# The last inverse DFT of a gated FFT mixer in two halves of 256 columns in place of two quarters and a half, with the MLP's result added sooner

## The chip, the cores and the metric

One core of one Trainium2 chip runs the whole kernel in one launch. The metric is the device time of that launch in microseconds, and a change counts as faster or slower when it moves the time by over 2%. In a profile the span, from the first to the last instruction, is some 2 us shorter than the time of the same run.

The engines are named as the profile names them: PE is TensorE (matmuls), PEld its weight loads, DVE is VectorE, ACT is ScalarE, POOL is GpSimd, SP is SyncE, whose queue issues the transfers. PSUM is the memory that matmuls write to; it has eight banks of 128 x 512 f32.

## The reference

A row of 512 features is mixed in two ways and the two results are blended with a gate. One way is a global filter (a 2D FFT over the 2048 rows and 512 features, a product with a complex weight, and the inverse FFT); the other is an MLP with the Mish activation.

```python
x = A_x                                              # 1 x 2048 x 512, bf16
g = sigmoid((x * gate_w).sum(-1, keepdims=True))
X = rfft2(x)                                         # over rows and features
a = irfft2(X * (w_r + 1j * w_i), (2048, 512)).astype(bf16)
h = einsum("bsd,df->bsf", x, w1) + b1                # 512 -> 1792
b = einsum("bsf,fd->bsd", h * tanh(softplus(h)), w2) # 1792 -> 512
out = g * a + (1 - g) * b
```

## The kernel before

The kernel is a list of small tasks (`G.add`). Each has one or two possible engines with an estimated duration, the tiles that it reads and writes, and a priority. A scheduler in the program puts them in order on each engine before anything is built, so the order of instructions follows from the list and its estimates; every engine then runs its list strictly in that order. The rows are 16 tiles of 128 (`t`).

The DFTs are matmuls with constant matrices. The forward part, the complex product (with a shuffle through DRAM on either side) and the MLP's first products come first. The stage that matters here is the last one, which runs beside the MLP. For each tile it does:

- the inner product (`s1i`): four matmuls of 128 columns against GT, into one PSUM bank;
- a copy of that bank to SBUF as bf16 (`e5`, tile TT), on ScalarE or VectorE;
- the outer product (`a1i`): matmuls of TT against GD, the inverse DFT along the features, into one PSUM bank (`sy`);
- the gate and the sum with the MLP's tile.

The inverse DFT along the features is folded. The frequencies k fall into even ones, with sum E, and odd ones, with sum O; both are needed for n < 256 only, as y(n) = E(n) + O(n) and y(n + 256) = E(n) - O(n). Before the change E is folded a second time: the frequencies that are multiples of four give C0 and the others C2, for n < 128 only, and E is C0 + C2 on the first 128 columns and C0 - C2 on the next. So the bank `sy` holds C0 (128 columns), C2 (128) and O (256).

```python
# inner product: weights are strided slices of T2r, 128 columns of GT move through
for i in range(4):
    st_ = T2r[:, 2*t:2*t+2, 2*i::4] if i < 2 else T2r[:, 2*t+i-2, 1::2]
    ins = e.matmul(ps[:, bk(sk), 128*i:128*(i+1)], st_, GT[:, t, :], start=True, stop=True)
... # e5: TT <- that bank
# outer product
for i in range(2):
    e.matmul(o[:, 128*i:128*i+128], TT[:, st.i, i, :], GD[:, 128*i:128*i+128], start=True, stop=True)
e.matmul(o[:, 256:512], TT[:, st.i, 2, :], GD[:, 256:512], start=True, stop=False)
return e.matmul(o[:, 256:512], TT[:, st.i, 3, :], GD[:, 512:768], start=False, stop=True)
...
# ge, on ScalarE (or VectorE):  tE[256:384] = g * C0
# ee, VectorE, twice 128:       tE[0:128] = g * C2 + g * C0 ; tE[128:256] = -g * C2 + g * C0
# yr, VectorE, twice 256:       d = g * O + tE ; d' = -g * O + tE
#     t < NEARLY (early): d is a bf16 scratch tile tA;  else d is the output tile ya
# yb, VectorE, early tiles only: ya = ya + tA
```

A tile of the MLP's result reaches the output in one of two ways. In an early tile (`t < NEARLY`, 12 of 16 before) the task `bev` copies the MLP's PSUM bank to `ya`, scaled with 1 - g (`omg`), and the filter's part is added later (`yb`). In a late tile the filter's part is in `ya` first, and the task `fo` adds the MLP's bank: `ya = omg * bank + ya`, on VectorE. The MLP's second product is `mm2` (14 matmuls of 512 columns per tile, in two groups of seven), its first one `mm1` (groups of four).

```python
fpool = _Pool(4)     # four PSUM banks for s1i and a1i together
mpool = _Pool(4)     # four for the MLP
ttpool, tepool = _Pool(3), _Pool(3)     # three TT and three tE tiles
```

Of the kernel before, what the change touches and what calls it, by code (L numbers as in the profile page):

```python
# [7 lines left out]
BF = mybir.dt.bfloat16  # L8
F32 = mybir.dt.float32
AF = mybir.ActivationFunctionType  # L10
ALU = mybir.AluOpType

S, D, F = 2048, 512, 1792
# [3 lines left out]
BIAS = 0.15  # L17
NWARM = 14
NTR = 4
NEARLY = 12  # L20


BGRP = {1: (0, 2), 3: (2, 2), 7: (4, 4), 11: (8, 4), 15: (12, 4)}
# [164 lines left out]
def _build_consts():  # L188
    cs = {}
    n = np.arange(128)[:, None]  # L190
    q = np.arange(64)[None, :]

    def trig(nn, k):
        th = 2 * np.pi * nn * k / D
        return np.cos(th), -np.sin(th)

    c0, s0 = trig(n, 4 * q)
    s0[:, 0] = (-1.0) ** np.arange(128)
    c2, s2 = trig(n, 4 * q + 2)
    ko = np.concatenate([4 * q + 1, 4 * q + 3], axis=1)  # L200
    blocks = [c0, s0, c2, s2]
    for h in range(2):
        c1, s1 = trig(n + 128 * h, ko)
        blocks += [c1, s1]
    cs["FD"] = np.concatenate(blocks, axis=1)

    p = np.arange(128)[:, None]
    e = np.arange(64)[None, :]
    FT = np.zeros((128, NT, 128))
    GT = np.zeros((128, NT, 128))  # L210
    for t in range(NT):
        th = 2 * np.pi * e * (16 * p + t) / S
        FT[:, t, 0:64] = np.cos(th)
        FT[:, t, 64:128] = -np.sin(th)
        FT[:, t, 64] = (-1.0) ** p[:, 0]
        GT[0:64, t, :] = 2 * np.cos(th).T
        GT[64:128, t, :] = -2 * np.sin(th).T
        GT[0, t, :] = 1.0
        GT[64, t, :] = (-1.0) ** p[:, 0]
    cs["CF"] = np.concatenate([cs.pop("FD"), FT.reshape(128, NT * 128)], axis=1)  # L220
    cs["GT"] = GT


    GD = np.zeros((128, 768))
    n1, n2 = np.arange(128)[None, :], np.arange(256)[None, :]
    for i in range(2):
        th = 2 * np.pi * (4 * np.arange(64)[:, None] + 2 * i) * n1 / D
        GD[0:64, 128 * i:128 * i + 128] = 2 * np.cos(th)
        GD[64:128, 128 * i:128 * i + 128] = -2 * np.sin(th)
    GD[0, 0:128] = 1.0  # L230
    GD[64, 0:128] = (-1.0) ** np.arange(128)
    th = 2 * np.pi * (2 * np.arange(128)[:, None] + 1) * n2 / D
    GD[:, 256:512] = 2 * np.cos(th)
    GD[:, 512:768] = -2 * np.sin(th)
    cs["GD"] = GD / (S * D)
    cs["SM"] = _stage2()
    return cs
# [162 lines left out]
PR = dict(ld=100.0, tr=99.5, a1=98.0, s1=99.0, mid=96.0, fin=94.0, mm1=80.0, act=90.0, mm2=70.0, out=95.0, gate=99.8, cp=95.5, gx=97.0)  # L400


def _build(nc, A_x, A_w_r, A_w_i, B_w1, B_b1, B_w2, gate_w, out):
# [5 lines left out]
    G = _Graph()  # L409
    es = ExitStack()  # L410
    with es:
        def sb(name, shape, dt):
            return es.enter_context(nc.sbuf_tensor(name, shape, dt))
# [8 lines left out]
        hsb = sb("hsb", [128, 3, NFT, 512], BF)  # L422
        CF = sb("CF", [128, 768 + NT * 128], BF)
        FD = CF[:, 0:768]
        GD = sb("GD", [128, 768], BF)
        FT = CF[:, 768:].rearrange("p (t e) -> p t e", t=NT)
        GT = FT
        SM = sb("SM", [128, len(MATS), 128], BF)
# [4 lines left out]
        PX = PXf.bitcast(BF)  # L433
# [14 lines left out]
        Xb = PX[:, 0:1024].rearrange("p (i k) -> p i k", i=2)  # L448
        P1 = PX[:, 1024:2048].rearrange("p (i k) -> p i k", i=2)
        P2 = PX[:, 2048:3072].rearrange("p (i k) -> p i k", i=2)  # L450
        tA = PX.rearrange("p (i k) -> p i k", i=3)
        tE = PXf[:].rearrange("p (i k) -> p i k", i=3)
        x_sb = R1[:].rearrange("p (t d) -> p t d", t=NT)
        In2 = R2[:].rearrange("p (j k) -> p j k", j=32)
# [36 lines left out]
        def bk(s):  # L491
            return s.i if s.pool is fpool else 4 + s.i
# [14 lines left out]
        def pe_dur(ncols, nmm=1):  # L507
            return nmm * max(ncols / 2400.0 + 0.003, 0.057)

        def act_dur(n, ptr=False):  # L510
            return 0.17 + n * 0.000833 + (0.09 if ptr else 0.0)

        def dve_dur(n, rate=1.0, ptr=False):
            return 0.15 + n * 0.001042 / rate + (0.06 if ptr else 0.0)
# [17 lines left out]
        G.add("eul", [("pool", 0.2, lambda e: e.memset(eul[:, :], float(np.e)))], writes=["eul"], prio=99)  # L532


        G.add("zero", [("dve", 0.2, lambda e: e.memset(GD[:, 0:512], 0.0))], writes=["GD"], prio=100)  # L535
        sl = fslot()
        for i in range(NWARM):
            G.add(f"warm{i}", [("pe", 0.42 if i < 5 else 0.22, lambda e, sl=sl: e.matmul(ps[:, bk(sl), :], GD[:, 0:128], GD[:, 0:512], start=True, stop=True))],  # L538
                  reads=["GD"], writes=[sl], slots=[sl] if i == 0 else (), prio=-100.0)


# [178 lines left out]

        for t in range(8, NT):
            ld_xt(t, t_r1r)
        dma("ld_gd", GD[:], d_c["GD"][:], 128 * 1536, writes=["GD"], deps=t_r1r)
        dma("ld_gt", GT, d_c["GT"][:], 128 * 4096, writes=["GT"], deps=t_s1 + t_r1r)


# [151 lines left out]
        for t in range(NT):  # L878
            sk = fslot()

            def f_s1i(e, t=t, sk=sk):
                ins = None
                for i in range(4):
                    st_ = T2r[:, 2 * t:2 * t + 2, 2 * i::4] if i < 2 else T2r[:, 2 * t + i - 2, 1::2]
                    ins = e.matmul(ps[:, bk(sk), 128 * i:128 * (i + 1)], st_, GT[:, t, :], start=True, stop=True)  # L885
                return ins

            G.add(f"s1i_{t}", [("pe", pe_dur(128, 4), f_s1i)], reads=[("T2r", t // 4), "GT"], writes=[sk], slots=[sk], deps=t_a1i[t - 3:t - 2] if t > 2 else (), prio=PR["fin"])
            st = _Slot(ttpool)

            def f_e5(e, sk=sk, st=st):
                return e.tensor_copy(out=TT[:, st.i, :, :].rearrange("p a b -> p (a b)"), in_=ps[:, bk(sk), :])  # L892

            def f_e5a(e, sk=sk, st=st):
                return e.activation(TT[:, st.i, :, :].rearrange("p a b -> p (a b)"), ps[:, bk(sk), :], AF.Copy)  # L895

            G.add(f"e5_{t}", [("dve", dve_dur(512), f_e5), ("act", act_dur(512), f_e5a)], reads=[sk], writes=[st], slots=[st], prio=PR["fin"] + 0.2)
            sy = fslot()

            def f_a1i(e, st=st, sy=sy):  # L900
                o = ps[:, bk(sy), :]
                for i in range(2):
                    e.matmul(o[:, 128 * i:128 * i + 128], TT[:, st.i, i, :], GD[:, 128 * i:128 * i + 128], start=True, stop=True)  # L903
                e.matmul(o[:, 256:512], TT[:, st.i, 2, :], GD[:, 256:512], start=True, stop=False)  # L904
                return e.matmul(o[:, 256:512], TT[:, st.i, 3, :], GD[:, 512:768], start=False, stop=True)  # L905

            t_a1i.append(G.add(f"a1i_{t}", [("pe", pe_dur(128, 2) + pe_dur(256, 2), f_a1i)], reads=[st, "GD"], writes=[sy], slots=[sy], prio=PR["fin"] + 0.3))
            se = _Slot(tepool)
            G.add(f"ge_{t}", [("act", act_dur(128, True), lambda e, t=t, sy=sy, se=se: e.activation(tE[:, se.i, 256:384], ps[:, bk(sy), 0:128], AF.Copy, scale=gcol[:, t:t + 1])),  # L909
                              ("dve", dve_dur(128, ptr=True), lambda e, t=t, sy=sy, se=se: e.tensor_scalar(  # L910
                                  out=tE[:, se.i, 256:384], in0=ps[:, bk(sy), 0:128], scalar1=gcol[:, t:t + 1], scalar2=None, op0=ALU.mult))],
                  reads=[sy, "gcol"], writes=[se], slots=[se], prio=PR["fin"] + 0.4)

            def f_ee(e, t=t, sy=sy, se=se):
                for o, g in ((0, gcol), (128, ngcol)):
                    ins = e.scalar_tensor_tensor(out=tE[:, se.i, o:o + 128], in0=ps[:, bk(sy), 128:256], scalar=g[:, t:t + 1], in1=tE[:, se.i, 256:384], op0=ALU.mult, op1=ALU.add)
                return ins

            G.add(f"ee_{t}", [("dve", 2 * dve_dur(128, ptr=True), f_ee)], reads=[sy, "gcol", "ngcol"], writes=[se], prio=PR["fin"] + 0.4)
            early = t < NEARLY  # L920

            def f_yr(e, t=t, sy=sy, se=se, early=early):
                for o, g in ((0, gcol), (256, ngcol)):
                    d = tA[:, se.i, 512 + o:768 + o] if early else ya[:, t, o:o + 256]
                    ins = e.scalar_tensor_tensor(out=d, in0=ps[:, bk(sy), 256:512], scalar=g[:, t:t + 1], in1=tE[:, se.i, 0:256], op0=ALU.mult, op1=ALU.add)  # L925
                return ins

            G.add(f"yr_{t}", [("dve", 2 * dve_dur(256, ptr=True), f_yr)], reads=[sy, "gcol", "ngcol"] + ([] if early else [se]),
                  writes=[se] if early else [("ya", t)], deps=t_r1w, prio=PR["fin"] + 0.4)
            if early:  # L930
                G.add(f"yb_{t}", [("dve", dve_dur(512, 2), lambda e, t=t, se=se: e.tensor_tensor(  # L931
                    out=ya[:, t, :], in0=ya[:, t, :], in1=tA[:, se.i, 512:1024], op=ALU.add))],
                      reads=[se, ("b", t)], writes=[("o", t, 0)], prio=PR["fin"] + 0.4)

        for t, n0, n1, sl in late:
            def f_out(e, t=t, sl=sl, n0=n0, n1=n1):
# [116 lines left out]
```

## Time and profile before

| what | before |
|---|---|
| time, median of 3 (lowest, highest) | 135.46 us (135.18, 135.64) |
| span of the profiled execution | 133.5 us |
| TensorE busy | 128.9 us |
| VectorE busy | 99.4 us |
| ScalarE busy | 82.8 us |
| mean TensorE clock, of full | 1.00 |
| copy of a bank after s1i on ScalarE, 128 x 512 | 593 ns |
| scaled copy on ScalarE (`ge`), 128 x 128 | 364 ns |
| `ee`, one of its two, 128 x 128 | 345 ns |
| `yr`, one of its two, 128 x 256 | 484 ns |
| `yb`, 128 x 512, bf16 in and out | 426 ns |
| `fo`, 128 x 512 | 752 ns |

The duration of a matmul in a group is from its start to its modelled end (219 ns for 128 columns), and neighbours overlap. What a matmul costs in a dense stream is read from the distances in the chain of waits, not from that mean. The busy time of a group counts overlaps once.

Lines of the kernel that the profile names: L836 is `mm1`, L858 `mm2`, L869 `bev`, L885 `s1i`, L892 and L895 its copy on VectorE and on ScalarE, L903 to L905 `a1i`, L909 and L910 `ge` on ScalarE and on VectorE, L916 `ee`, L925 `yr`, L931 `yb`, L937 `fo`. L521 and L520 are the copies out of PSUM of the earlier stages, on ScalarE and on VectorE, and L809 is a matmul of the stage before.

### The profile page before, as it was taken

The page shows a single profiled execution, that of the slowest core. Times are in us where ns is not written, and L with a number is a line of the kernel's source. Part 1 is how long each engine was busy: PE and PEld are TensorE (multiplying, and loading weights), DVE is VectorE, ACT ScalarE, POOL GpSimd, SP SyncE. Part 2 cuts the span into 40 slices and gives each one's busy share as a digit, 9 for nine tenths or more (in the row PEclk, how much of TensorE's full clock was granted, in tenths as well). Part 3 has the DMA queues.
Part 4 walks back from the last instruction along what each step waited for, and adds up shares of the span by engine and source line. Part 5 has one row for each costly group of instructions (what it writes and reads, how often), then busy time and mean ns, then how long its engine had stood idle before and what let it go on. Part 6 is the DMA issues. An engine that isn't in the chain of part 4 may idle for free.

```text
span 133.5 us, 2357 instructions
## 1 busy us (share of the span) xinstructions
PE 128.9 (97%) x813; PEld 69.4 (52%) x813; DVE 99.4 (75%) x241; ACT 82.8 (62%) x145; POOL 4.7 (4%) x8
## 2 busy tenths in 40 slices
PE   6999999999999999999998999999999999999991
PEld 2489565675444444444443444445666566565451
DVE  0558868487999799999999995001899999977822
ACT  3199788896774156756167898778887654552000
POOL 2000000000002900000000000000000000000000
PEclk9999999999999999999999999999999999999999
DMA  3999999997999999947100840399311222220121
GB/s 89 289 382 401 329 187 158 190 333 230 254 352 394 383 166 125 140 100 206 49 0 0 323 158 0 158 258 290 80 46 37 79 79 79 79 85 1 43 75 39
DMA packets 25015, 22.24 MB, mean 167 GB/s; under 512 B 7596, under 2 KB 21420, under 8 KB 24876
## 3 DMA queue, kind: packets, MB, share of 16 engines
q1 hardware_dynamic: 24976, 22.10, 62.2%
q8 instruction: 6, 0.10, 0.3%
q14 instruction: 5, 0.04, 0.1%
q10 hardware_dynamic: 28, 0.00, 0.0%
HBM read 14.23 MB, written 6.29 MB: 154 GB/s over the span
## 4 chain that ended last, share of the span: by engine, by line
PE 45%; DVE 5%; issue 1%; ACT 0%; ACTq 0%
PE ps L858 18%; PE ps L836 18%; PE ps L885 3%; PE ps L903 1%; PE ps L904 1%; PE ps L905 1%; PE ps L809 1%; DVE PX L794 1%; DVE PX L793 1%; DVE Wb L692 1%; DVE PX L790 1%; DVE PX L797 1%; PE ps L780 1%; DVE R L520 1%; ACT PX L521 0%
## 5 line engine op out<-in xcount | busy, mean ns | idle before, releaser
L836 PE MATMUL ps<-xT,w_sb 128*128 128x512 bf16 (+1 forms) x240 | 52.3, 365 | 0.1
L858 PE MATMUL ps<-w_sb,hsb 128*128 128x512 bf16 (+2 forms) x238 | 52.3, 366 | 0.0
L845 ACT ACTIVATE hsb<-ps,b1f 128x512 bf16<-128x512 f32 (+1 forms) x60 | 38.9, 660 | 9.4 <-PE ps L836 9.4
L858 PEld LDWEIGHTS ps<-w_sb,hsb 128*128 128x128 bf16 x238 | 22.3, 98 | 22.9
L836 PEld LDWEIGHTS ps<-xT,w_sb 128*128 128x128 bf16 x240 | 22.7, 98 | 22.0 <-issue 0.6
L520 DVE CAST R<-ps 128x512 bf16<-128x512 f32 (+1 forms) x23 | 15.4, 689 | 6.6 <-PE ps L656 3.7
L521 ACT ACTIVATE R<-ps 128x512 bf16<-128x512 f32 (+1 forms) x25 | 14.4, 595 | 3.1 <-PE ps L809 2.1
L869 ACT ACTIVATE R<-ps,omg 128x512 bf16<-128x512 f32 x12 | 8.1, 687 | 9.2 <-PE ps L858 8.1
L521 ACT ACTIVATE PX<-ps 128x512 bf16<-128x512 f32 x15 | 8.9, 596 | 6.9 <-PE ps L779 4.1
L699 DVE SCALAR_TENSOR_TENSOR R<-R,gwb 128x512 bf16<-128x512 bf16 x16 | 9.9, 687 | 0.2 <-DVE R L520 0.2
L909 ACT ACTIVATE PX<-ps,gcol 128x128 f32<-128x128 f32 x15 | 5.4, 364 | 5.7 <-PE ps L905 5.7
L892 DVE CAST TT<-ps 128x512 bf16<-128x512 f32 x2 | 1.3, 687 | 9.9 <-PE ps L885 9.9
L895 ACT ACTIVATE TT<-ps 128x512 bf16<-128x512 f32 x14 | 8.3, 593 | 0.2 <-PE ps L885 0.2
L797 DVE TENSOR_TENSOR PX<-PX 128x512 bf16<-128x512 bf16 x16 | 6.8, 424 | 1.0
L793 DVE TENSOR_TENSOR PX<-PX,Wb 64x512 bf16<-64x512 bf16 x16 | 6.7, 421 | 0.5
L794 DVE TENSOR_TENSOR PX<-PX,Wb 64x512 bf16<-64x512 bf16 x16 | 6.7, 420 | 0.2
L790 DVE TENSOR_TENSOR PX<-PX,Wa 128x512 bf16<-128x512 bf16 x16 | 6.8, 423 | 0.1
L538 PE MATMUL ps<-GD 128*128 128x512 bf16 x14 | 5.6, 527 | 1.2 <-DVE GD L535 1.2
L809 PE MATMUL ps<-PX,SM 128*128 128x512 bf16 x15 | 5.7, 380 | 0.6 <-ACT PX L521 0.6
L925 DVE SCALAR_TENSOR_TENSOR PX<-ps,gcol,PX 128x256 bf16<-128x256 f32 x12 | 5.8, 484 | 0.5
L937 DVE SCALAR_TENSOR_TENSOR R<-ps,omg,R 128x512 bf16<-128x512 f32 (+2 forms) x5 | 3.2, 645 | 3.9 <-PE ps L858 3.9
L931 DVE TENSOR_TENSOR R<-R,PX 128x512 bf16<-128x512 bf16 x12 | 5.1, 426 | 1.2 <-ACT R L869 0.8
(98 smaller groups left out, 127.9 us busy)
## 6 DMA issues: line engine op xcount, KB each, us to landing
scr<-R SPq DMA_DIRECT2D x8, 512.0 KB, 4.0
R<-scr SPq DMA_DIRECT2D x8, 512.0 KB, 7.4
w_sb<-in_B_w_dram SPq DMA_DIRECT2D x2, 896.0 KB, 7.8
out_dram<-R SPq DMA_DIRECT2D x7, 256.0 KB, 2.0
R<-in_A_x_dram SPq DMA_DIRECT2D x3, 512.0 KB, 9.6
w_sb<-in_B_w_dram SPq DMA_DIRECT2D x1, 1280.0 KB, 7.7
SM<-c_sm SPq DMA_DIRECT2D x1, 576.0 KB, 6.3
Wa<-in_A_w_r_dram SPq DMA_DIRECT2D x2, 257.0 KB, 8.1
```

The source lines that it names most:

```text
L520: t = G.add(name, [("dve", dve_dur(n), lambda e: e.tensor_copy(out=outf(), in_=inf())), ("act", act_dur(n), lambda e: e.activation(outf(), ...
L521: ("act", act_dur(n), lambda e: e.activation(outf(), inf(), AF.Copy))],
L699: t_gx.append(G.add(f"gx{t}", [("dve", 0.72, lambda e, t=t: e.scalar_tensor_tensor(out=x_sb[:, t, :], in0=x_sb[:, t, :], scalar=1.0, in1=g ...
L790: return e.tensor_tensor(out=v(P1, sP, 0, 128), in0=v(Xb, sX, 0, 128), in1=Wa[:, js, 0:256], op=ALU.mult)
L793: e.tensor_tensor(out=v(P2, sQ, 0, 64), in0=v(Xb, sX, 64, 128), in1=Wb[64:128, js, 0:256], op=ALU.mult)
L794: return e.tensor_tensor(out=v(P2, sQ, 64, 128), in0=v(Xb, sX, 0, 64), in1=Wb[0:64, js, 0:256], op=ALU.mult)
L797: return e.tensor_tensor(out=P1[:, sP.i, :], in0=P1[:, sP.i, :], in1=P2[:, sQ.i, :], op=ALU.add)
L836: ins = e.matmul(ps[:, bk(sl), cols], w1_sb[:, dt_, 128 * ft:128 * (ft + 1)], xT[:, dt_, 4 * c + h0:4 * c + h1, :], start=(dt_ == 0), stop ...
L845: return e.activation(hsb[:, hb, ft, cols], ps[:, bk(sl), cols], AF.Mish, bias=b1f[:, ft:ft + 1])
L858: ins = e.matmul(ps[:, bk(sl), 0:n1 - n0], hsb[:, hb, ft, 128 * tl:128 * (tl + 1)], w2_sb[:, ft, n0:n1], start=(ft == 0), stop=(ft == NFT ...
L869: G.add(f"bev_{t}", [("act", act_dur(512, True), lambda e, t=t, sl=sl: e.activation(ya[:, t, :], ps[:, bk(sl), :], AF.Copy, scale=omg[:, t ...
L895: return e.activation(TT[:, st.i, :, :].rearrange("p a b -> p (a b)"), ps[:, bk(sk), :], AF.Copy)
```

## The change

The second fold is taken away. E is computed at full width, 256 columns from 128 even frequencies (K is 128 for the cosine part and 128 for the sine part), just as O is. The bank `sy` then holds E (256 columns) and O (256), and `ee`, the two instructions that put E together, falls away. The weights of the inner product are sliced with a step of two throughout. The constant matrix GD grows from 768 to 1024 columns.

The early tiles are eight in place of twelve. In an early tile `ge` now does more: it reads E twice, by a broadcast, and adds the MLP's tile in the same instruction, and `yr` (now `ya`) writes the output, so that `yb` falls away too. In the late tiles, eight in place of four, `bev` falls away and `fo` comes in.

The aim is fewer instructions on VectorE and ScalarE per tile. The loads of x and of the filter's weights are the same in both versions.

```diff
-NEARLY = 12
+NEARLY = 8
...
-        GD = sb("GD", [128, 768], BF)
+        GD = sb("GD", [128, 4, 256], BF)
...
-        dma("ld_gd", GD[:], d_c["GD"][:], 128 * 1536, writes=["GD"], deps=t_r1r)
+        dma("ld_gd", GD[:], d_c["GD"][:], 128 * 2048, writes=["GD"], deps=t_r1r)
...
                 for i in range(4):
-                    st_ = T2r[:, 2 * t:2 * t + 2, 2 * i::4] if i < 2 else T2r[:, 2 * t + i - 2, 1::2]
-                    ins = e.matmul(ps[:, bk(sk), 128 * i:128 * (i + 1)], st_, GT[:, t, :], start=True, stop=True)
+                    pl, hh = i % 2, i // 2
+                    ins = e.matmul(ps[:, bk(sk), 128 * i:128 * (i + 1)], T2r[:, 2 * t + pl, hh::2], GT[:, t, :], start=True, stop=True)
...
-                o = ps[:, bk(sy), :]
-                for i in range(2):
-                    e.matmul(o[:, 128 * i:128 * i + 128], TT[:, st.i, i, :], GD[:, 128 * i:128 * i + 128], start=True, stop=True)
-                e.matmul(o[:, 256:512], TT[:, st.i, 2, :], GD[:, 256:512], start=True, stop=False)
-                return e.matmul(o[:, 256:512], TT[:, st.i, 3, :], GD[:, 512:768], start=False, stop=True)
+                for i in range(4):
+                    hh = i // 2
+                    ins = e.matmul(ps[:, bk(sy), 256 * hh:256 * (hh + 1)], TT[:, st.i, i, :], GD[:, i, :], start=(i % 2 == 0), stop=(i % 2 == 1))
...
-            # ge (ACT or DVE, 128 columns), ee (DVE, 2 x 128), yr (DVE, 2 x 256),
-            # and for t < NEARLY yb (DVE, 512)
+            if t < NEARLY:
+                # ge, DVE: tE = g * E (read twice by a broadcast) + ya, 512 columns
+                    return e.scalar_tensor_tensor(out=o, in0=ps[:, bk(sy), 0:256].unsqueeze(1).to_broadcast([128, 2, 256]), scalar=gcol[:, t:t + 1],
+                                                  in1=ya[:, t, :].rearrange("p (h n) -> p h n", h=2), op0=ALU.mult, op1=ALU.add)
+                # ya, DVE, 2 x 256: ya = g * O + tE[0:256] ; ya' = -g * O + tE[256:512]
+            else:
+                # ge (ACT or DVE, 256 columns): tE = g * E
+                # yr, DVE, 2 x 256: ya = g * O + tE ; ya' = -g * O + tE
```

The lines with a # inside the diff stand for code that was cut.

More of the change, by code (lines that the diff above doesn't have):

```diff
@@ L221, in _build_consts @@
     cs["GT"] = GT
-    GD = np.zeros((128, 768))
-    n1, n2 = np.arange(128)[None, :], np.arange(256)[None, :]
-    for i in range(2):
[L227 to L234, printed above, removed]
+    nn = np.arange(256)[None, :]
+    GD = np.zeros((128, 4, 256))
+    ke = 2 * np.arange(128)[:, None]
+    ko = ke + 1
+    for h, kk in enumerate((ke, ko)):
+        th = 2 * np.pi * kk * nn / D
+        GD[:, 2 * h, :] = 2 * np.cos(th)
+        GD[:, 2 * h + 1, :] = -2 * np.sin(th)
+    GD[0, 0, :] = 1.0
+    GD[0, 1, :] = (-1.0) ** np.arange(256)
     cs["GD"] = GD / (S * D)
@@ L450, in _build @@
         P2 = PX[:, 2048:3072].rearrange("p (i k) -> p i k", i=2)
-        tA = PX.rearrange("p (i k) -> p i k", i=3)
         tE = PXf[:].rearrange("p (i k) -> p i k", i=3)
@@ L532, in _build @@
         G.add("eul", [("pool", 0.2, lambda e: e.memset(eul[:, :], float(np.e)))], writes=["eul"], prio=99)
-        G.add("zero", [("dve", 0.2, lambda e: e.memset(GD[:, 0:512], 0.0))], writes=["GD"], prio=100)
+        GDf = GD[:].rearrange("p i k -> p (i k)")
+        G.add("zero", [("dve", 0.2, lambda e: e.memset(GDf[:, 0:512], 0.0))], writes=["GD"], prio=100)
         sl = fslot()
         for i in range(NWARM):
-            G.add(f"warm{i}", [("pe", 0.42 if i < 5 else 0.22, lambda e, sl=sl: e.matmul(ps[:, bk(sl), :], GD[:, 0:128], GD[:, 0:512], start=True, stop=True))],
+            G.add(f"warm{i}", [("pe", 0.42 if i < 5 else 0.22, lambda e, sl=sl: e.matmul(ps[:, bk(sl), :], GDf[:, 0:128], GDf[:, 0:512], start=True, stop=True))],
                   reads=["GD"], writes=[sl], slots=[sl] if i == 0 else (), prio=-100.0)
@@ L900, in f_a1i @@
             def f_a1i(e, st=st, sy=sy):
-                o = ps[:, bk(sy), :]
[L902 to L907, printed above, removed]
@@ L908, in _build @@
-            se = _Slot(tepool)
[L909 to L933, printed above, removed]
+                ins = None
@@ new lines, in f_a1i, with f_ge, f_ya, f_yr @@
+                for i in range(4):
+                    hh = i // 2
+                    ins = e.matmul(ps[:, bk(sy), 256 * hh:256 * (hh + 1)], TT[:, st.i, i, :], GD[:, i, :], start=(i % 2 == 0), stop=(i % 2 == 1))
+                return ins
+            t_a1i.append(G.add(f"a1i_{t}", [("pe", pe_dur(256, 4), f_a1i)], reads=[st, "GD"], writes=[sy], slots=[sy], prio=PR["fin"] + 0.3))
+            se = _Slot(tepool)
+            if t < NEARLY:
+                def f_ge(e, t=t, sy=sy, se=se):
+                    o = tE[:, se.i, :].rearrange("p (h n) -> p h n", h=2)
+                    return e.scalar_tensor_tensor(out=o, in0=ps[:, bk(sy), 0:256].unsqueeze(1).to_broadcast([128, 2, 256]), scalar=gcol[:, t:t + 1],
+                                                  in1=ya[:, t, :].rearrange("p (h n) -> p h n", h=2), op0=ALU.mult, op1=ALU.add)
+                G.add(f"ge_{t}", [("dve", dve_dur(512, ptr=True), f_ge)], reads=[sy, "gcol", ("b", t)], writes=[se], slots=[se], prio=PR["fin"] + 0.4)
+                def f_ya(e, t=t, sy=sy, se=se):
+                    e.scalar_tensor_tensor(out=ya[:, t, 0:256], in0=ps[:, bk(sy), 256:512], scalar=gcol[:, t:t + 1], in1=tE[:, se.i, 0:256], op0=ALU.mult, op1=ALU.add)
+                    return e.scalar_tensor_tensor(out=ya[:, t, 256:512], in0=ps[:, bk(sy), 256:512], scalar=ngcol[:, t:t + 1], in1=tE[:, se.i, 256:512], op0=ALU.mult, op1=ALU.add)
+                G.add(f"ya_{t}", [("dve", 2 * dve_dur(256, ptr=True), f_ya)], reads=[sy, se, "gcol", "ngcol"],
+                      writes=[("o", t, 0)], prio=PR["fin"] + 0.4)
+            else:
+                G.add(f"ge_{t}", [("act", act_dur(256, True), lambda e, t=t, sy=sy, se=se: e.activation(tE[:, se.i, 0:256], ps[:, bk(sy), 0:256], AF.Copy, scale=gcol[:, t:t + 1])),
+                                  ("dve", dve_dur(256, ptr=True), lambda e, t=t, sy=sy, se=se: e.tensor_scalar(
+                                      out=tE[:, se.i, 0:256], in0=ps[:, bk(sy), 0:256], scalar1=gcol[:, t:t + 1], scalar2=None, op0=ALU.mult))],
+                      reads=[sy, "gcol"], writes=[se], slots=[se], prio=PR["fin"] + 0.4)
+                def f_yr(e, t=t, sy=sy, se=se):
+                    e.scalar_tensor_tensor(out=ya[:, t, 0:256], in0=ps[:, bk(sy), 256:512], scalar=gcol[:, t:t + 1], in1=tE[:, se.i, 0:256], op0=ALU.mult, op1=ALU.add)
+                    return e.scalar_tensor_tensor(out=ya[:, t, 256:512], in0=ps[:, bk(sy), 256:512], scalar=ngcol[:, t:t + 1], in1=tE[:, se.i, 0:256], op0=ALU.mult, op1=ALU.add)
+                G.add(f"yr_{t}", [("dve", 2 * dve_dur(256, ptr=True), f_yr)], reads=[sy, se, "gcol", "ngcol"], writes=[("ya", t)], deps=t_r1w, prio=PR["fin"] + 0.4)
```

## The prediction

> **What bounds the kernel now.** I read the head of the page and its forty slices first, to find the engine that has no air.
>
> ```profile
> span 133.5 us, 2357 instructions
> PE 128.9 (97%) x813; PEld 69.4 (52%) x813; DVE 99.4 (75%) x241; ACT 82.8 (62%) x145; POOL 4.7 (4%) x8
> ...
> PE   6999999999999999999998999999999999999991
> ...
> DVE  0558868487999799999999995001899999977822
> ACT  3199788896774156756167898778887654552000
> ```
>
> TensorE is busy 97% of the span. VectorE is dense as well in slices 30 to 36, where the changed code runs, and a busy share does not say which of the two sets the end. So I read the chain of waits next, in order of time (start, length, what ran). From 71.20 us to the last matmul it holds matmuls and nothing else. One round of the changed stage (outer product L903 to L905, inner product L885, a group of the MLP L836), then the end:
>
> ```profile
> 94.74 0.11 PE ps L903 x2
> 94.85 0.11 PE ps L904
> 94.96 0.11 PE ps L905
> 95.07 0.22 PE ps L885 x4
> 95.29 1.73 PE ps L836 x8
> 97.02 0.11 PE ps L903 x2
> ...
> 121.69 9.12 PE ps L858 x56
> 130.80 0.02 issue
> 130.83 0.35 DVE R L937
> ```
>
> So from 71 us on every matmul starts when the one before it has streamed, and the list of who waited for whom has no wait of TensorE on a line of this stage (the largest there, 0.6 us, is at L809, before it). VectorE, ScalarE and the transfers are hidden behind it. A cost added to TensorE here is paid in full; work taken off VectorE or ScalarE is worth nothing unless it was about to hold TensorE up.
>
> **What the Trainium skill says.** "TensorE: Matmul & The Clock Gate", section "Wait — 56ns, not 53.3ns?": back-to-back matmuls start N/2.4 + 2.5 ns apart, so 56 ns at 128 columns and 109 ns at 256. The chain agrees: two of 128 columns take 0.11, one of 256 takes 0.11. The same page, "Step-by-step: what each phase is for": matmuls stay in program order and only weight loads are pulled ahead. So a matmul that must wait delays every one behind it, also those of the MLP. "VectorE: DVE Perf Modes", section "Mode 1× (REGULAR) — the baseline": with a PSUM operand VectorE makes one result per cycle, whatever the type. The groups agree: between 128 and 512 columns (345 and 752 ns, below) the slope is 407/384 = 1.06 ns per element, with f32 or bf16 in and out. So I may take durations of new shapes from that line.
>
> **The change, part by part.** *TensorE, the outer product (a1i).* Per tile of 128 rows, 128 + 128 + 256 + 256 = 768 columns become 4 x 256 = 1024. From the chain: 0.11 + 0.11 + 0.11 = 0.33 us becomes 4 x 0.11 = 0.44. Sixteen tiles: 16 x 0.11 = **+1.77 us** (with 109.2 and 55.6 ns: 16 x 2 x (109.2 - 55.6) = 1.72). All of it is on the chain. *The inner product (s1i)* keeps 4 x 128 columns; only the stride of its weights goes from four elements to two. Its weight loads take 105 ns at the wider stride against 98 ns elsewhere, and four matmuls still take 0.22 in the chain: nothing to win.
>
> *VectorE and ScalarE.* The groups of the stage before:
>
> ```profile
> L925 DVE SCALAR_TENSOR_TENSOR PX<-ps,gcol,PX 128x256 bf16<-128x256 f32 x12 | 5.8, 484 | 0.5
> L916 DVE SCALAR_TENSOR_TENSOR PX<-ps,gcol,PX 128x128 f32<-128x128 f32 x16 | 5.5, 345 | 0.0
> L909 ACT ACTIVATE PX<-ps,gcol 128x128 f32<-128x128 f32 x15 | 5.4, 364 | 5.7 <-PE ps L905 5.7
> L931 DVE TENSOR_TENSOR R<-R,PX 128x512 bf16<-128x512 bf16 x12 | 5.1, 426 | 1.2 <-ACT R L869 0.8
> L937 DVE SCALAR_TENSOR_TENSOR R<-ps,omg,R 128x512 bf16<-128x512 f32 x3 | 2.3, 752 | 2.2 <-PE ps L858 2.2
> ```
>
> VectorE before: twelve early tiles x (345 + 343 + 484 + 476 + 426) = 24.9 us, four late ones x (345 + 343 + 482 + 475) = 6.6, evacuations at L937 3.2, one scaled copy 0.35: 35.0 us. After: eight early tiles x (752 + 484 + 476) = 13.7, eight late x (482 + 475) = 7.7, nine evacuations 7 x 0.752 + 0.62 + 0.35 = 6.2, and, by the order of instructions as built, two of the scaled copies x 0.48 = 1.0: 28.6 us. So **6.4 us come off VectorE**. ScalarE loses 15 copies of 364 ns (5.5) and four of 687 (2.7) and gets six of about 470 (2.8): **5.4 us off**. Both lay beside TensorE, so I count them as 0.
>
> *What the change moves.* Because the schedule is made anew, the order on TensorE differs in this stage alone. Before, each tile from the fourth on had seven or eight MLP matmuls (1.51 or 1.73 us) or more between its inner and its outer product. Now tiles 3 to 7 have four (0.86). Between the two products ScalarE copies the result out of PSUM. What that takes, from the timeline (start, length):
>
> ```profile
> 100.55 0.39 PE L885 MATMUL ps<-CF,R 128*128 128x128 bf16 x4
> ...
> 100.98 0.60 ACT L895 ACTIVATE TT<-ps 128x512 bf16<-128x512 f32 x1 [0.21 <-PE ps L885]
> ```
>
> The copy starts 0.43 after the inner product and lasts 0.60. TensorE picks up about 0.13 after such a copy: at L809, the copy at L521 started at 70.46, took 0.60, and the matmul ran at 71.20, 0.14 later. Needed: 0.43 + 0.60 + 0.13 = 1.16 us. There is 0.22 + 0.86 = 1.08. A wait of 0.08 us for five tiles: **+0.4 us**. Against that stands VectorE's pace. An early tile takes 0.78 (752 ns, and the next one depends on it) + 0.40 + 0.40 = 1.58 us between starts (the timeline has 0.40 between neighbours at L925); TensorE's round is now 0.22 + 0.86 + 0.44 + 0.08 = 1.60. So PSUM banks come free just in time. From the ninth tile on, with 1.51 us of MLP per one or two tiles, I find one to two us of slack.
>
> *The rest.* The matrix GD grows from 192 to 256 KB; its fetch is issued at 60.1 us and lands 3.3 us later, some 30 us ahead of its use. The end (the last MLP matmul, L937 on 128 columns, a store) is as before.
>
> Sum: 135.46 + 1.77 + 0.4 = 137.6; as the second term is the soft one, I say **137.5 us**, a ratio of 1.015.
>
> **The rivals.** *VectorE held the end, and 6 us less of it shortens the kernel.* For it: slices 31 to 35 of VectorE are nines. Against it: no matmul of this stage waited, and VectorE itself idles before L937 (2.2 us for TensorE). If it were so, the time would fall by up to 6.4 - 1.8 = 4.6 us, to about 131. I give it 2 in 100. *VectorE becomes the pace of tiles 3 to 7.* 1.58 against 1.60 is close; if the instruction that reads one half of a bank twice (the broadcast) or adds a bf16 tile took 0.9 in place of 0.75, each of these rounds would be 0.13 longer, and the banks' slack of some 0.5 us would be eaten after four tiles: up to 0.8 us more, 138.3. *The wait on the copy is hidden after all*, because ScalarE answers faster or four buffers give the room: then 1.77 alone remains, 137.2. *The slack that VectorE gains lets TensorE run denser*: it cannot, as its stage has no gaps.
>
> **Range and chances.** The floor is the streaming alone, 137.2, and the spread of the time before (135.18 to 135.64) adds 0.3 on either side. The top has both waits, about 138.3. Range 136.9 to 138.3. The border of 2% is 138.17. Faster by over 2%: 0.02. Within 2%: 0.86. Slower by over 2%: 0.12.
>
> **What would show it.** Right: the outer product's four matmuls stand at 0.44 in the chain; TensorE's busy time goes to about 130.7; VectorE's falls to about 93 and ScalarE's to about 77; the matmuls of the outer product wait for ScalarE's copy about 0.1 us at a time, in five tiles; the chain from 71 us on stays TensorE's. Wrong: a wait on VectorE at an outer product of over 0.3 us in all, a 512-column L910 well over 0.75 us, or a stretch before 92 us that differs, where neither the work nor its order was touched.

## The result, and the profile after

| what | before | after |
|---|---|---|
| time, median of 4 | 135.37 us | 137.30 us |
| ratio, 95% interval | | 1.0139 (1.0119 to 1.0159) |
| span of the profiled execution | 133.5 us | 135.6 us |
| TensorE busy | 128.9 us | 131.1 us |
| VectorE busy | 99.4 us | 94.5 us |
| ScalarE busy | 82.8 us | 79.0 us |

The changed kernel is slower by 1.4%, within the 2% that count as the same. The two engines that the change was to relieve are relieved; the one that sets the end has more to do. The head of the page after, with the slices of the two engines:

```profile
span 135.6 us, 2286 instructions
PE 131.1 (97%) x813; PEld 70.6 (52%) x813; DVE 94.5 (70%) x210; ACT 79.0 (58%) x132; POOL 4.7 (3%) x8
...
PE   6999999999999999999998999999999999999992
...
DVE  0548868487999799999999993003999978842222
ACT  3199788786773166676167898777675554400000
```

VectorE's and ScalarE's last digits have fallen to twos and noughts. TensorE's row has not one digit less than before. The chain of waits in order of time (start, length, what ran), two rounds of the stage and the end; L902 is now the outer product, L883 the inner one, L834 and L856 the MLP:

```profile
95.77 0.22 PE ps L883 x4
95.99 0.86 PE ps L834 x4
96.85 0.48 PE ps L902 x4
97.34 0.22 PE ps L883 x4
97.56 0.86 PE ps L834 x4
98.42 0.44 PE ps L902 x4
...
117.78 15.16 PE ps L856 x84
132.93 0.02 issue
132.96 0.35 DVE R L935
```

Four matmuls of 256 columns take 0.44 us where two of 128 and two of 256 took 0.33. The first of these two rounds has 0.48, so one wait of 0.04; the other rounds have none. The groups of the new instructions (columns as in the prediction):

```profile
L910 DVE SCALAR_TENSOR_TENSOR PX<-ps,gcol,R 128x512 f32<-128x512 f32 x8 | 5.9, 744 | 0.5 <-PE ps L902 0.5
L916 DVE SCALAR_TENSOR_TENSOR R<-ps,gcol,PX 128x256 bf16<-128x256 f32 x8 | 3.9, 484 | 0.3
L922 ACT ACTIVATE PX<-ps,gcol 128x256 f32<-128x256 f32 x6 | 2.8, 474 | 5.7 <-PE ps L902 5.7
L935 DVE SCALAR_TENSOR_TENSOR R<-ps,omg,R 128x512 bf16<-128x512 f32 x7 | 5.3, 750 | 8.6 <-PE ps L856 8.5
```

The fused instruction L910, which reads half a bank twice, takes 744 ns, as long as L935, which reads 512 different columns (750): that the columns are read twice makes no difference. L935 shows where the freed time of VectorE went: it waited 8.5 us for matmuls.

To compare runs closely I use one length in all that follows: from the first matmul at L809 in the chain after 71 us (L807 after the change) to the start of the last VectorE instruction. It is 130.83 - 71.20 = **59.63 us before and 132.96 - 71.58 = 61.38 us after: 1.75 us more**. What lies ahead of it is the same program in both, and there the profile after is 0.38 us later. Each stage below comes from one profiled execution.

### The profile page after: what moved, and what is told of

Read it like the earlier page. It is cut to its first block, busy times and chain, and to the rows that moved or that the text cites. A ratio compares the mean times of both kernels' runs of the same rounds, so it can differ in the third digit from the quotient of the medians.

```text
span 135.6 us, 2286 instructions
## 1 busy us (share of the span) xinstructions
PE 131.1 (97%) x813; PEld 70.6 (52%) x813; DVE 94.5 (70%) x210; ACT 79.0 (58%) x132; POOL 4.7 (3%) x8
## 4 chain that ended last, share of the span: by engine, by line
PE 45%; DVE 5%; issue 1%; ACT 0%; ACTq 0%
PE ps L856 18%; PE ps L834 18%; PE ps L902 5%; PE ps L883 3%; PE ps L807 1%; DVE PX L792 1%; DVE PX L791 1%; DVE Wb L690 1%; DVE PX L788 1%; DVE PX L795 1%; PE ps L778 1%; DVE R L517 1%; ACT PX L518 0%; DVE R L935 0%; PE ps L759 0%
## 5 line engine op out<-in xcount | busy, mean ns | idle before, releaser
L834 PE MATMUL ps<-xT,w_sb 128*128 128x512 bf16 (+1 forms) x240 | 52.6, 365 | 0.0
L856 PE MATMUL ps<-w_sb,hsb 128*128 128x512 bf16 (+2 forms) x238 | 51.6, 366 | 0.0
L856 PEld LDWEIGHTS ps<-w_sb,hsb 128*128 128x128 bf16 x238 | 22.5, 98 | 23.8
L834 PEld LDWEIGHTS ps<-xT,w_sb 128*128 128x128 bf16 x240 | 22.6, 98 | 21.1 <-issue 0.2
L935 DVE SCALAR_TENSOR_TENSOR R<-ps,omg,R 128x512 bf16<-128x512 f32 (+2 forms) x9 | 6.2, 692 | 10.3 <-PE ps L856 10.2
L893 ACT ACTIVATE TT<-ps 128x512 bf16<-128x512 f32 x14 | 8.0, 595 | 2.7 <-PE ps L883 2.7
L902 PE MATMUL ps<-GD,TT 128*128 128x256 bf16 x64 | 8.8, 272 | 0.0
L867 ACT ACTIVATE R<-ps,omg 128x512 bf16<-128x512 f32 x8 | 5.4, 687 | 5.7 <-PE ps L856 4.6
L902 PEld LDWEIGHTS ps<-GD,TT 128*128 128x128 bf16 x64 | 5.9, 98 | 3.5 <-ACT TT L893 1.6
L536 PE MATMUL ps<-GD 128*128 128x512 bf16 x14 | 6.1, 564 | 1.2 <-DVE GD L533 1.2
L910 DVE SCALAR_TENSOR_TENSOR PX<-ps,gcol,R 128x512 f32<-128x512 f32 x8 | 5.9, 744 | 0.5 <-PE ps L902 0.5
L807 PE MATMUL ps<-PX,SM 128*128 128x512 bf16 x15 | 5.7, 380 | 0.6 <-ACT PX L518 0.6
```

The source lines that it names most:

```text
L834: ins = e.matmul(ps[:, bk(sl), cols], w1_sb[:, dt_, 128 * ft:128 * (ft + 1)], xT[:, dt_, 4 * c + h0:4 * c + h1, :], start=(dt_ == 0), stop ...
L856: ins = e.matmul(ps[:, bk(sl), 0:n1 - n0], hsb[:, hb, ft, 128 * tl:128 * (tl + 1)], w2_sb[:, ft, n0:n1], start=(ft == 0), stop=(ft == NFT ...
L902: ins = e.matmul(ps[:, bk(sy), 256 * hh:256 * (hh + 1)], TT[:, st.i, i, :], GD[:, i, :], start=(i % 2 == 0), stop=(i % 2 == 1))
```

## Experiments

All ratios are to the kernel before, with their 95% intervals; "stage" is the length just defined.

| run | what it has | ratio (interval) | stage, us | against |
|---|---|---|---|---|
| x1_cols_only | 1024 columns, twelve early tiles | 1.0102 (1.0065 to 1.0140) | 61.32 | before +1.69 |
| x2_border_only | 768 columns, eight early tiles | 0.9977 (0.9950 to 1.0005) | 59.63 | before +0.00 |
| x3_cols_back | the change at 768 columns | 1.0017 (0.9995 to 1.0040) | 60.02 | after -1.36 |
| x4_cols_more | the change at 1536 columns | 1.0396 (1.0361 to 1.0431) | 64.82 | after +3.44 |
| x5_slow_copy | the change, ScalarE's copy slower | 1.0155 (1.0117 to 1.0193) | 61.63 | after +0.25 |
| x6_dve_pad | the change, VectorE padded | 1.0152 (1.0117 to 1.0187) | 61.88 | after +0.50 |
| x7_before_pad | before, VectorE padded | 1.0033 (1.0015 to 1.0052) | 60.05 | before +0.42 |
| x8_after_again | the change once more | 1.0121 (1.0088 to 1.0154) | 61.38 | after +0.00 |

**The columns alone.** The changed kernel with the border back at twelve and the sum of before in the early tiles:

```diff
-NEARLY = 8
+NEARLY = 12
-    # early tile: ge on VectorE, 512 columns, + ya ; then ya = +-g * O + tE
+    # early tile: ge = g * E on ScalarE, 256 columns ; yr = +-g * O + tE into tA ;
+    #             yb: ya = ya + tA
```

> The outer product at 1024 columns as in the changed kernel, but twelve early tiles and the sum with the MLP's tile as before (scaled copy, two of 256 columns, and the 512-column addition); the two 128-column instructions fall away with the second fold. Theory (TensorE streams without gaps, so its columns are the cost): 16 x 0.11 = 1.8 us above before, 137.2, the same as the changed kernel within 0.4 us. Rival (the cost comes from the moved border or the fused instruction with the broadcast, and not from the columns): within 0.5 us of before, 135.4.

The stage is 61.32 us, 1.69 more than before and 0.06 less than after. With the border and the fused instruction undone the cost is still there: it belongs to the columns. The median of the whole time was lower than expected (136.54 us, where 137.2 was named), though the profiled execution took 137.21. I put that down to the start of an execution (x8, below); it is not shown, as the others have no profile.

**The border alone.**

```diff
-NEARLY = 12
+NEARLY = 8
```

> The kernel before with eight early tiles in place of twelve and nothing else: four copies of the MLP's bank leave ScalarE, four 512-column sums leave VectorE and four evacuations come in. Theory: nothing of it is on TensorE, so 135.4, the same as before within 0.3 us. Rival: the border costs by itself, 1 to 2 us more, as the MLP's banks come free later.

The stage is 59.63 us, to the hundredth that of before. ScalarE's busy time fell from 82.8 to 80.7 us and VectorE's rose from 99.4 to 100.8, and no matmul of the stage waits for either.

**The columns taken back.** The second quarter of E (its columns 128 to 255) is left out and the first is read in its place, in the late tiles too (not shown):

```diff
-ins = e.matmul(ps[:, bk(sy), 256*hh:256*(hh+1)], TT[:, st.i, i, :], GD[:, i, :], ...)
+n = 256 if hh else 128
+ins = e.matmul(ps[:, bk(sy), 256*hh:256*hh+n], TT[:, st.i, i, :], GD[:, i, 0:n], ...)
-in0=ps[:, bk(sy), 0:256].unsqueeze(1).to_broadcast([128, 2, 256])
+in0=ps[:, bk(sy), 0:128].unsqueeze(1).to_broadcast([128, 4, 128])
```

> The changed kernel in which the even half E is computed for its first 128 columns only and these are read again for the other 128 (the second quarter of E is left out): 768 columns as before, order of instructions as in the changed kernel, VectorE and ScalarE as in the changed kernel. Theory: the 1.8 us go away, but rounds 3 to 7 of TensorE are then 0.22 + 0.86 + 0.33 = 1.41 us against 1.57 of VectorE, so that up to 0.4 us come back as waits for PSUM banks: 135.5 to 135.9. Rival (the wait for ScalarE's copy and the order cost, not the columns): over 136.5.

The time, 135.33 us, lies just under the 135.5 to 135.9 that I had named. In the stage 1.36 us of the 1.75 are gone, and 0.39 stay as waits, as expected. Its chain shows where (L903 is the outer product here):

```profile
95.59 0.10 issue
95.69 0.49 PE ps L903 x4
...
100.12 0.33 PE ps L903 x4
100.45 0.33 PE ps L883 x4
```

A free round has 0.33 for L903 and 0.22 for L883. At 95.59 the outer product waited 0.10 and then took 0.49, together 0.26 too long; that is the first tile with only four MLP matmuls between its products. What it waited for is read from the timeline (in brackets the idle time and what the view gives as its end):

```profile
94.76 0.60 ACT L893 ACTIVATE TT<-ps 128x512 bf16<-128x512 f32 x1 [0.53 <-PE ps L883]
95.06 0.47 DVE L918 SCALAR_TENSOR_TENSOR R<-ps,ngcol,PX 128x256 bf16<-128x256 f32 x1
...
95.66 0.24 PEld L903 LDWEIGHTS ps<-GD,TT 128*128 128x128 bf16 x4 [0.56 <-ACT TT L893]
```

The view names L893, ScalarE's copy, but that ended at 95.36, 0.30 before the load. L918 on VectorE ended at 95.53, 0.13 before it; this is the last to read the first tile's PSUM bank, and by the order of the tasks this outer product writes into that bank. At 100.45 the inner product took 0.11 too long, and there the timeline names L918 itself. So it is VectorE that TensorE waits for: with fewer columns TensorE's round (1.41 us) is shorter than VectorE's (1.57), which frees the banks, and so the change with its order of instructions would not have gained even at the old number of columns.

**Twice the extra columns, and more.** The two matmuls of E are issued twice:

```diff
-                for i in range(4):
+                for i in (0, 1, 0, 1, 2, 3):
```

> The changed kernel with the two matmuls of E issued twice (the first pair is overwritten): 512 columns more per tile, 1536 in all. Theory: 16 x 2 x 0.109 = 3.5 us more, 140.8, a slope of 0.43 ns per column as between before and after. Rival (part of the columns fits into gaps of TensorE): under 2 us more.

The stage grew by 3.44 us, and the wait of 0.04 is gone from it: 3.48 us for 16 x 512 columns, 0.42 ns per column. From before to after it was 1.75 us with that wait, so 1.71 for 16 x 256 columns, 0.42 ns per column again. The two steps lie on one straight line: TensorE had no gap in which columns fit. A round here (a longer outer product gives more time to all the rest, and no wait is left):

```profile
97.84 0.86 PE ps L834 x4
98.71 0.66 PE ps L902 x6
```

**The wait for ScalarE's copy.**

```diff
-return e.activation(TT[:, st.i, :, :].rearrange("p a b -> p (a b)"), ps[:, bk(sk), :], AF.Copy)
+e.activation(TT[:, st.i, 0:2, :].rearrange("p a b -> p (a b)"), ps[:, bk(sk), 0:256], AF.Copy)
+return e.activation(TT[:, st.i, 2:4, :].rearrange("p a b -> p (a b)"), ps[:, bk(sk), 256:512], AF.Copy)
```

> The changed kernel, in which ScalarE copies the inner product's bank in two instructions of 256 columns in place of one of 512; all else, the order too, is the same. In the changed kernel's trace 0.43 (until the copy starts) + 0.60 (copy) + 0.06 (pick-up) = 1.09 us fit exactly into 0.22 + 0.86 of TensorE's work in rounds 3 to 7. Theory (no slack there): each of these five rounds gets longer by what the pair takes beyond 0.60 us; at 0.7 to 0.8 us for the pair the stage grows by 0.5 to 1.0 us, and TensorE's loads wait that much longer for ScalarE. Rival (the copy is hidden with slack to spare): under 0.2 us.

The pair takes less than I had assumed: 0.28 or 0.29 until the second starts and 0.38 for it, 0.66 to 0.67 us, 0.06 to 0.07 more than the one copy. The timeline of one round (start, length):

```profile
97.61 0.38 ACT L893 ACTIVATE TT<-ps 128x256 bf16<-128x256 f32 x1
...
97.90 0.38 ACT L894 ACTIVATE TT<-ps 128x256 bf16<-128x256 f32 x1
...
98.33 0.61 PE L903 MATMUL ps<-GD,TT 128*128 128x256 bf16 x4
```

The stage grew by 0.25 us: in the chain all five rounds have 0.50 for the outer product, where after the change four have 0.44 and the first 0.48. My span of 0.5 to 1.0 was missed because the pair was cheaper, but every further hundredth of the copy was paid in full, as the theory without slack says; the rival had under 0.2.

**VectorE padded after the change.** One product that nobody uses, 291 ns long and 0.21 between starts, in each of the eight early tiles:

```diff
 def f_ya(e, t=t, sy=sy, se=se):
+    e.tensor_tensor(out=gwb[:, 0:256], in0=gwb[:, 256:512], in1=gwb[:, 256:512], op=ALU.mult)
```

> The changed kernel with one useless VectorE product of 128x256 bf16 (about 0.22 us between starts) in each of the eight early tiles: VectorE's round goes from 1.57 to about 1.79 us against 1.52 of TensorE, 1.8 us of VectorE in all. Theory (VectorE is off the path but is the next to bind, with 0.4 to 0.5 us of slack in PSUM banks in rounds 5 to 7): TensorE waits for banks, the stage grows by about 0.45 us. Rival A (VectorE has the freed 5 us to give): 0. Rival B (VectorE is the bound): 1.8 us.

The stage grew by 0.50 us, close to the 0.45 expected: 1.7 us of VectorE cost 0.5 us of time. The largest of its waits:

```profile
101.60 0.24 PEld L883 LDWEIGHTS ps<-CF,R 128*128 128x128 bf16 x4 [0.34 <-DVE R L918]
```

L918 is the last instruction that reads a bank of the outer product, and the inner product needs that bank. This place cost 0.25 us, the inner product one tile before 0.06, and the outer product at 96.32 cost 0.21. At that one the view names ScalarE's copy, but the copy had ended 0.28 before the load and L918 0.12 before it, so it is the bank again, as in x3. Both rivals fall: four of the products, 0.84 us, come before the wait shown and were more than VectorE had to give, and the other four cost nothing more, so it isn't the bound either.

**VectorE padded before the change.** The same product in all sixteen tiles:

```diff
 def f_yr(e, t=t, sy=sy, se=se, early=early):
+    e.tensor_tensor(out=gwb[:, 0:256], in0=gwb[:, 256:512], in1=gwb[:, 256:512], op=ALU.mult)
```

> The kernel before with the same useless product in each of the sixteen tiles: 3.5 us more on VectorE, whose round goes from 1.89 to 2.11 us against 2.06 of TensorE. Theory (VectorE did not set the end before the change): under 0.4 us. Rival (VectorE set it, so that taking work off it should have helped): 2 us or more.

Sixteen times 0.21 us are 3.4 us more of VectorE, and the stage grew by 0.42 us, just over the 0.4 that I had allowed. So the kernel before was not bound by VectorE: its chain has no wait for it, and 4.9 us less of it could not have helped. But it stood near. The 0.42 us come at one place, the inner product of tile 6:

```profile
100.81 0.24 PEld L885 LDWEIGHTS ps<-CF,R 128*128 128x128 bf16 x4 [0.73 <-DVE PX L926]
```

L926 reads the bank that it needs. In the kernel before that bank was free 0.18 us ahead (its last reader ends at 100.23, the pick-up takes 0.14, the inner product starts at 100.55). All that follows on TensorE, the MLP's matmuls too, came 0.42 us later. A round of VectorE with the product is 2.09 us against 2.06 of TensorE.

**The change once more.** No edit.

> The changed kernel once more, beside the others on the same chip. Theory: 1.0130 of before (1.75 us of matmul columns), from the first matmul of L807 to the last of all 61.35 us; what differs from execution to execution lies in the first 10 us[...]. Rival (the 0.38 us by which L807 starts later after the change belong to the change): L807 starts at 71.5 us or later again, ratio 1.0155.

The stage is 61.38 us again. L807 starts at 71.22 us, not at 71.58, and the ratio is 1.0121. So the 0.38 us ahead of the stage are not the change's. In all ten profiles the first matmul of the forward DFT starts between 8.85 and 9.79 us, and from there to L807 (or L809) it is 61.78 to 61.81 us in each. What differs between executions of one program lies in the first 10 us. In the profile with the earliest start the 14 matmuls that fill this time have a mean of 495 ns, in the one with the latest 564.

## Why the prediction was right, and where it was not

- **TensorE is the bound.** Right. The chain is its own before and after; 3.4 us more for VectorE cost 0.42 us before the change (x7), four fewer copies on ScalarE moved nothing (x2).
- **The outer product, +1.77 us.** Right, and nearly the whole cost: 61.38 - 59.63 - 0.04 = 1.71. Of the prediction's two sums the finer one, 1.72 (an estimate with 109.2 and 55.6 ns), is the nearer; 16 x 0.11 is 1.76, not 1.77. That the columns are the cause was shown by adding them without the rest (x1, +1.69), by taking them back (x3) and by adding more (x4, the same slope).
- **The inner product's stride, nothing to win.** Right: its weight loads went from 105 to 98 ns, and its four matmuls take 0.22 us still. The 105 is the mean of all its loads before, of which half already had a step of two.
- **6.4 us off VectorE and 5.4 off ScalarE, worth 0.** The worth is right. The sizes were 4.9 and 3.8 in busy time, as I had summed durations, which overlap by some 0.08 us between neighbours, where the busy time counts an overlap once.
- **A wait of 0.08 us in five tiles, +0.4.** This term was mis-sized: ScalarE's copy held up no outer product, in none of the five tiles. The step that failed is "TensorE picks up about 0.13 after such a copy", which I had taken from a single place, L809. In the stage itself it was 0.06. The first of the five rounds and the second, in the timeline after:

```profile
96.03 0.60 ACT L893 ACTIVATE TT<-ps 128x512 bf16<-128x512 f32 x1 [0.84 <-PE ps L883]
96.12 0.48 DVE L917 SCALAR_TENSOR_TENSOR R<-ps,ngcol,PX 128x256 bf16<-128x256 f32 x1
...
96.71 0.35 PEld L902 LDWEIGHTS ps<-GD,TT 128*128 128x128 bf16 x4 [0.35 <-ACT TT L893]
...
97.17 0.39 PE L883 MATMUL ps<-CF,R 128*128 128x128 bf16 x4
...
97.60 0.60 ACT L893 ACTIVATE TT<-ps 128x512 bf16<-128x512 f32 x1
...
98.25 0.33 PEld L902 LDWEIGHTS ps<-GD,TT 128*128 128x128 bf16 x4 [0.32 <-ACT TT L893]
98.26 0.60 PE L902 MATMUL ps<-GD,TT 128*128 128x256 bf16 x4
```

  In the second round the copy starts 0.43 after the inner product, as predicted, ends at 98.20, and the matmul runs at 98.26. That makes 1.09 us, and TensorE has 1.08. The weight load waits 0.32 us, which looks like a loss, but a load that is early anyway may wait: the matmul behind it was not later. Only where the copy is made longer is it paid (x5). Why L809 took 0.14 was not tried.

  The 0.04 us that were measured lie in the first round, and by the distances they are a wait for a bank. The load follows the copy's end (96.63) by 0.08 there, and by 0.05 in the four other rounds; it follows the end of L917, the last to read the first tile's bank, by 0.11. In x3 and x6, where this wait is longer, it followed VectorE by 0.13 and 0.12.
- **VectorE's pace, 1.58 against 1.60.** Right for VectorE: L910 starts every 1.57 us in the timeline after. TensorE's round is 1.52, without the wait that I had counted in, so VectorE falls behind by 0.05 a tile. As this runs for few tiles only, the slack in PSUM banks covered it, but for the 0.04 above. I had put that at some 0.5 us; at the tightest place, the inner product of tile 7, it is 0.30 (the last reader of the bank ends at 101.31, the pick-up from VectorE takes 0.14 as in x6, the inner product starts at 101.75). Four tiles with 0.21 more each overrun it by 0.54, where x6 measured 0.50.
- **The time, 137.5 us.** Measured 137.3, with the two terms 1.71 and 0.04, where I had 1.77 and 0.4. That the prediction lay 0.2 us off and not 0.4 is in part luck: the profiled execution after started its stage 0.38 us late, and the repeat, at 137.06 us, is nearer to the sum of the measured terms, 135.37 + 1.71 + 0.04 = 137.12.

No run beat both kernels: the intervals of x2 and x3 include 1. As TensorE's stream in this stage has no gap, a faster version would need fewer columns in it.

## What to carry to other kernels

Before you trade matmul columns for instructions on another engine, ask the chain which of the two ends last: a saturated TensorE pays each added column in full (0.42 ns here), and 5 us saved on an engine behind it bring nothing. And a scheduler spends what was freed: after the change it packed TensorE's rounds tighter (1.52 us where they had 2.06 or more), so VectorE stood about as close to binding as before, with less to do: it caused one wait of 0.04 us and had 0.30 to spare at the tightest inner product, where before it caused none and had 0.18. Last, where a view names what ended a wait, look when that was done: twice it named a copy that had ended 0.3 us before, and the wait was for a bank.

## What the runs showed of the hardware that was not expected

A VectorE instruction that reads 256 columns of PSUM twice by a broadcast and adds a bf16 tile takes 744 ns, as much as one that reads 512 columns once (750). Two ScalarE copies of 256 columns back to back take 0.66 to 0.67 us where one of 512 takes 0.60: the second start follows 0.28 or 0.29 us after the first, though each is reported with 0.38. In this stage TensorE's weight load began 0.05 us after the end of a ScalarE copy that it waited for (four rounds of the profile after), and 0.11 to 0.13 us after that of a VectorE instruction (after, x3, x6, x7). And the length of the saturated stage was the same to 0.01 us in the repeat (61.38), while the first 10 us, the same program in all ten profiles, moved by up to 0.9.
